# Attention forward and backward on one core: head strips at 32 rows, a shorter query-major exponential with DMA transposes for the rest, and gradient scores placed around the burst

## The chip, the cores and the metric

The kernel runs on one core of a Trainium2 chip. The time is device microseconds of one execution; the kernel before takes 2680.48 us in the median of 3 runs (2678.87 to 2681.03). The core has a matrix engine (PE, which loads weights through PEld), a vector engine (DVE), an activation engine (ACT), a general engine (POOL) and a queue engine (SP); DMA transfers are issued from SP, ACT and POOL.

## The reference

One layer mixes two branches with a gate, and the kernel returns the output and the gradients of eleven inputs. Only branch A matters here: attention over 2048 positions with 32 heads of width 18, forward and backward. The other branch, a state-space convolution, matters by one thing: its basis tables are built on POOL while the attention runs.

```python
g = sigmoid((x * gate_w).sum(-1, keepdims=True))
qkv = (x @ wqkv)                                # 32 heads, head width 18
scores = einsum("bhqd,bhkd->bhqk", q, k) * 18**-0.5
o = einsum("bhqk,bhkd->bhqd", softmax(scores), v)
out = g * (o @ wo) + (1 - g) * B(x, ...)        # B: the convolution branch
_out, _vjp = jax.vjp(f, A_x, A_wqkv, A_wo, ..., gate_w);  _grads = _vjp(grad_out)
```

## The kernel before

**Stages.** A first stage projects q, k and v and writes them to a DRAM tensor `QKV_d` as strips, one row for each head channel, 2048 positions long. The attention follows (from about 120 to 2100 us), then the convolution branch and the output projections.

**Units and steps.** Four heads form a group and occupy 32 partitions each. A *unit* is one group and one block of 512 queries; there are 8 groups x 4 blocks = 32 units (`NU`). A unit has 32 *steps* (`NST`); the loop over `G` runs through 1024 steps (`NTOT`), and the backward half trails the forward half by `OFF` = 39 steps, so one step works on two units at once:

- *P1*: scores with keys on partitions, for 128 keys, 512 queries and two heads. ACT turns them into exponentials, tile `PT` (L1388).
- *P3*: scores with queries on partitions, for 128 queries, 512 keys (block `kq`) and two heads. ACT turns them into exponentials, tile `eb` (L1393).
- *P2*: gradient scores, one for each of two heads; DVE multiplies each with `PT` into tile `ds` (L1398).
- the *burst*: one of eight slots, repeated for each `kq`: the gradient of V from `eb` and `dOa` (two halves, `dv_half`), of Q from `ds` (two halves), of K from `dsT` (two halves), and two slots that transpose on PE (`turn`). A second half or a turn ends with an eviction on DVE (`evs`).
- in half of the steps, four matmuls of the forward output `accO`.

`dsT` is `ds` transposed, for the most part by DMA transposes issued from SP (L1406). The K, V and Q tiles (`KaT`, `VaT`, `QaT`, `Vtok`, `Ktok`, `Qtok`) and the packing transposes `gT` are on the same SP queue.

**Order.** The program is written out by hand (`manual_schedule`): each engine takes its instructions in the order in which the loop body emits them, and waits at the first one that isn't ready. `at(("pre", G), f)` emits `f` ahead of step `G`. PSUM holds two P1/P3 tiles (tag `S`), two P2 tiles (tag `dP`), one burst accumulator (`accB`) and `accO`.

**Between forward and backward of a unit.** DVE takes the reciprocal `rl` (L1044) of the row sums; POOL multiplies `dOa` (L1049) and `prod` (L1051); DVE reduces `prod` (L1057), PE turns `dOa`, and P2 of that unit can begin.

**POOL.** Besides these two multiplications POOL builds the tables of the convolution branch: a fixed list of multiplications and additions (L506), their stores (`E_d<-Eo`, L559), and the packing of gradients (`dtk`, L1075, stored at L1076). `e_emit` spreads the list over the steps: at each `G` it emits as much as a cost estimate says is due. What it emits stands in POOL's queue ahead of the next unit's `dOa`.

Of the kernel before, what the change touches and what calls it, by code (L numbers as in the profile page):

```python
# [17 lines left out]
P = 128  # L18


def build(tc, aps, dbg_aps=None, stages=("s1", "attn", "post", "s4", "final")):
# [23 lines left out]
    HS = DH + 2  # L45
    assert HS <= HP and (4 * HS) % 16 == 0
# [15 lines left out]
    with ExitStack() as gctx:  # L62
# [14 lines left out]

        HR = H * HS
        QKV_d = dram.tile([2 * HR + H * HP, S], BF, name="QKV_d")
        ROW0 = {"K": 0, "V": HR, "Q": 2 * HR}  # L80
        WID = {"K": HS, "V": HS, "Q": HP}
# [44 lines left out]
        woT = [eds.tile([P, 2, 512], BF, tag="eb", bufs=8, name="eb").rearrange("p a b -> p (a b)")[:, 0:D] for _ in range(DC)]  # L126
        dO_st = [eds.tile([P, 2, 512], BF, tag="eb", bufs=8, name="eb") for _ in range(3)]

        with ExitStack() as ctx:
# [11 lines left out]
            rows = [QKV_d[ROW0[k_]:ROW0[k_] + H * WID[k_], :].rearrange("(h w) s -> h w s", w=WID[k_]) for k_ in "QKV"]  # L141
# [48 lines left out]
            def load_const():  # L190
                for q_, (y0, y1) in enumerate(((DH + 1, HP), (DH, HS), (DH, HS))):
                    nc.sync.dma_start(rows[q_][:, y0:y1, :], cst_d[q_:q_ + 1].unsqueeze(1).to_broadcast([H, y1 - y0, S]))
# [757 lines left out]
        if "attn" in stages:  # L950
# [3 lines left out]
            DA = HP  # L954
            NFILL = {"V": 1, "Q": 0, "K": 0}
            with ExitStack() as ctx:
# [28 lines left out]
                def strip(k, g, c0, n):  # L985

                    r0 = ROW0[k] + 4 * g * WID[k]
                    return bass.AP(tensor=QKV_d.tensor, offset=QKV_d[r0:r0 + 1, c0:c0 + 1].offset, ap=[[WID[k] * S, 4], [S, HP], [1, n]])

# [12 lines left out]
                def load_piece(nm, g, m):  # L1002
# [4 lines left out]
                    else:  # L1007
                        t_ = ga.tile([P, TPQ, P], BF, tag=nm, bufs=PB[nm], name=nm + "_g")
                        r0 = ROW0[k] + 4 * g * WID[k]
# [126 lines left out]
                def dv_half(g, b, kq, h, acc):  # L1136
                    U = UN[(g, b)]
                    for ii in (2 * h, 2 * h + 1):
                        for j in range(4):
                            mm(acc[HP * j:HP * (j + 1), :], lhsT=U["dOa"][:, ii, j, :], rhs=U["eb"].pop((kq, ii, j)),  # L1140
                               start=(ii == 0), stop=(ii == 3), tile_position=(0, HP * j))

# [11 lines left out]
                def dq_half(g, b, kq, h, acc):  # L1154
                    U = UN[(g, b)]
                    for n_ in (2 * h, 2 * h + 1):
                        for j in range(4):
                            mm(acc[HP * j:HP * (j + 1), :], lhsT=grp_t[g]["Ktok", kq][:, n_, HS * j:HS * j + HP], rhs=U["ds"][TPQ * kq + n_][:, j, :],
# [83 lines left out]
                at(("pre", 4), load_z01)  # L1242
# [632 lines left out]
```

## Time and profile before

| | |
|---|---|
| median of 3 runs | 2680.48 us |
| span of the profiled execution | 2673.6 us |
| mean granted TensorE clock | 0.968 |
| busy, of the span | PE 90%, DVE 86%, ACT 88%, POOL 68%, PEld 42% |
| from 400 to 700 us | PE 270.34, DVE 272.21, ACT 300.00, POOL 253.68 of 300 us |

The profiled execution's own time isn't listed apart from the three runs; its span, from the first to the last instruction, is 2673.6 us, 6.9 us less than their median. Busy shares are means over stages: in the attention ACT has no idle time, and in the stages behind it ACT has little to do. A row of the chain of waits gives a start, a length and what was running. A row of a timeline gives start, length, engine, line, operation, tiles and, in brackets, the idle time before it with what ended it. Instructions overlap in the pipeline of an engine, so the pace of a row of equal instructions is the distance of their starts, which is shorter than the length of one.

### The profile page before, as it was taken

What the parts mean: (1) busy time and instruction counts of PE and PEld (TensorE: products, weight loads), DVE (VectorE), ACT (ScalarE), POOL (GpSimd) and SP (SyncE); (2) the same over time, 40 slices, a digit from 0 to 9 for tenths busy, and PEclk for the clock granted to TensorE, in tenths of its full rate; (3) what the DMA queues carried; (4) which work ended last, traced back from release to release, by engine and by line L of the source; (5) the groups of instructions that cost most, each with busy time, mean ns of one, the idle gap of its engine ahead of it and who ended that gap; (6) DMA issues with size and microseconds to landing.
All of it is one profiled execution on the core that took longest, in us unless ns stands there. A gap on an engine that the chain in (4) does not pass through costs nothing.

```text
span 2673.6 us, 69952 instructions
## 1 busy us (share of the span) xinstructions
PE 2405.5 (90%) x27411; PEld 1134.6 (42%) x27411; DVE 2294.7 (86%) x4090; ACT 2352.0 (88%) x2744; POOL 1830.1 (68%) x2845
## 2 busy tenths in 40 slices
PE   8999999998889898889898999989988699999999
PEld 4433333333333333333333333333232489998756
DVE  5748999999889999889899999999897499999964
ACT  5589999999999999999999999999996489999321
POOL 0388878888888888888878888887931135555431
PEclk9989999999999999999999999999896699999999
DMA  7747889879979978997898899779668979998996
GB/s 232 202 114 152 150 171 177 162 156 181 169 151 172 185 157 163 173 167 152 165 179 157 157 172 169 154 164 181 134 136 174 224 229 262 260 263 250 269 255 136
DMA packets 1155478, 486.63 MB, mean 182 GB/s; under 512 B 1071062, under 2 KB 1108551, under 8 KB 1152843
## 3 DMA queue, kind: packets, MB, share of 16 engines
q1 hardware_dynamic: 1108346, 339.13, 64.3%
q0 software_dynamic: 44784, 137.52, 19.2%
q10 hardware_dynamic: 2016, 5.51, 0.7%
q8 instruction: 214, 3.51, 0.6%
q14 instruction: 118, 0.96, 0.1%
HBM read 146.27 MB, written 93.80 MB: 90 GB/s over the span
## 4 chain that ended last, share of the span: by engine, by line
ACT 39%; PE 28%; DVE 22%; issue 6%; DMA 3%; POOL 2%; SPq 1%; ACTq 0%; DVEq 0%; POOLq 0%
ACT eb L1393 23%; ACT PT L1388 14%; PE ps_P L30 8%; DVE ds L1398 7%; DVE tz L733 3%; DVE wab L753 3%; PE accV L30 2%; PE ps_dx L30 2%; PE turn_p L1097 2%; DVE tz L736 2%; PE accK L30 2%; DVE HG L738 2%; PE yp L30 2%; DVE Rw L758 1%; DVE dvacc L1151 1%
## 5 line engine op out<-in xcount | busy, mean ns | idle before, releaser
L1398 DVE TENSOR_TENSOR ds<-ps_P,PT 128x512 bf16<-128x512 f32 x2048 | 1312.5, 683 | 127.8 <-PE ps_P L30 87.3
L1393 ACT ACTIVATE eb<-ps_P 128x1024 bf16<-128x1024 f32 x1024 | 1095.7, 1070 | 44.3 <-PE ps_P L30 44.2
L1388 ACT ACTIVATE PT<-ps_P 128x1024 bf16<-128x1024 f32 x1024 | 1099.6, 1075 | 11.0 <-PE ps_P L30 9.5
L30 PE MATMUL ps_P<-dOaT,VaT_g 32*128 32x512 bf16 x2048 | 583.1, 390 | 30.8 <-DVE ds L1398 15.4
L506 POOL TENSOR_TENSOR et<-eG,eT 128x448 f32<-128x448 f32 x576 | 542.9, 963 | 10.7
L30 PE MATMUL ps_P<-QaT_g,KaT_g 32*128 32x512 bf16 x2048 | 404.7, 387 | 126.6 <-ACT PT L1388 122.2
L30 PE MATMUL ps_P<-KaT_g,QaT_g 32*128 32x512 bf16 x2048 | 408.9, 392 | 2.0 <-ACT eb L1393 1.4
L506 POOL TENSOR_TENSOR Eo<-et,et 128x448 bf16<-128x448 f32 x288 | 327.2, 1136 | 20.8
L30 PEld LDWEIGHTS <-KaT_g 32*128 32x128 bf16 x2048 | 147.4, 91 | 456.1 <-issue 438.2
L30 PEld LDWEIGHTS <-QaT_g 32*128 32x128 bf16 x2048 | 115.7, 91 | 288.6 <-issue 266.7
L30 PE MATMUL accV<-eb,dOa 128*32 128x512 bf16 x2048 | 185.6, 396 | 26.8 <-ACT eb L1393 26.5
L30 PE MATMUL accO<-PT,Vtok_g 128*32 128x512 bf16 x2048 | 207.9, 395 | 0.1
L30 PE MATMUL accK<-dsT,Qtok_g 128*32 128x256 bf16 x4096 | 165.3, 283 | 21.3 <-DMA dsT<-ds 19.9
L30 PE MATMUL accQ<-ds,Ktok_g 128*32 128x512 bf16 x2048 | 161.9, 394 | 2.2 <-DVE dvacc L1151 1.9
L30 PEld LDWEIGHTS <-Vtok_g 128*32 128x32 bf16 x2048 | 52.8, 93 | 222.6 <-issue 222.6
L1102 DVE COPY dsT<-turn_p 128x1024 bf16<-128x1024 bf16 (+1 forms) x216 | 139.2, 644 | 3.4 <-PE turn_p L1097 3.4
L1097 PE MATMUL turn_p<-ident_bf,ds 128*128 128x128 bf16 x1664 | 136.2, 225 | 1.4 <-DVE gb L1169 0.8
L672 ACT COPY E1e<-etp 128x1024 bf16<-128x1024 bf16 x132 | 125.4, 1063 | 2.7 <-PE etp L671 2.7
L30 PEld LDWEIGHTS <-Qtok_g 128*32 128x32 bf16 x4096 | 88.6, 97 | 87.8 <-issue 57.9
L506 POOL TENSOR_TENSOR et<-eT 128x32 f32<-128x32 f32 (+3 forms) x288 | 116.2, 424 | 11.4
L1097 PEld LDWEIGHTS <-ds 128*128 128x128 bf16 x1664 | 98.9, 100 | 50.2 <-issue 50.0
L1075 POOL COPY dtk<-gT 128x288 bf16<-128x288 bf16 x96 | 40.9, 426 | 107.6 <-DMA dqkv_d<-dtk 47.2
(295 smaller groups left out, 3731.0 us busy)
## 6 DMA issues: line engine op xcount, KB each, us to landing
E_d<-Eo POOLq DMA_DIRECT2D x144, 256.0 KB, 3.3
E1n<-E_d POOLq DMA_DIRECT2D x30, 1024.0 KB, 6.6
T0w<-Kp_d SPq DMA_DIRECT2D x18, 1024.0 KB
xs<-xb_d POOLq DMA_DIRECT2D x28, 512.0 KB, 9.9
dsT<-ds SPq DMA_TRANSPOSE x512
dqkv_d<-dtk POOLq DMA_DIRECT2D x96, 72.0 KB, 4.3
Md_d<-mst SPq DMA_DIRECT2D x18, 288.0 KB
skw<-Md_d SPq DMA_DIRECT2D x72, 64.0 KB
```

The costliest lines, as they stand in the source:

```text
L30: return nc.tensor.matmul(out, lhsT=lhsT, rhs=rhs, start=start, stop=stop, **kw)
L506: nc.gpsimd.tensor_tensor(out, a, b, op=op)
L672: copy(E_[:, 4 * q:4 * q + 4], pt_)
L733: nc.vector.tensor_tensor(tz[x], HG[:, :, k - 1].unsqueeze(1).to_broadcast([P, 2, 2, n, CB]), ZZ.unsqueeze(3).to_broadcast([P, 2, 2, n, CB ...
L736: nc.vector.tensor_tensor(tz[x][:, 0], tz[x][:, 0], UVk[:, :, :, k, :], op=A.add)
L738: nc.vector.tensor_tensor(HG[:, :, k], tz[x][:, 0], tz[x][:, 1, ::-1], op=A.add)
L753: nc.vector.tensor_tensor(wab, h_, w_, op=A.mult)
L1097: nc.tensor.transpose(pt_[:, x, qb, :], t_[:, qb * P:(qb + 1) * P], ident_bf)
L1102: (nc.scalar.copy if NTOT <= now[0] < NTOT + OFF else nc.vector.tensor_copy)(o_(), pt_[:, x:x + n])
L1388: nc.scalar.activation(U["PT"][i, j // 2], ps, ACT.Exp)
L1393: nc.scalar.activation(e, ps, ACT.Exp)
L1398: nc.vector.tensor_tensor(U["ds"][i][:, j, :], ps, U["PT"][i, j // 2][:, j % 2, :], op=A.mult)
```

## The change

1. Heads in the K and V strips of `QKV_d` stand 32 rows apart (`HP`) rather than 20 (`HS`); `strip` becomes a plain block of 128 rows, and the slices of `Vtok` and `Ktok` move to multiples of 32. The added constant rows are written for the first four heads from SP, and for the other 28 by two DMAs from POOL at steps 8 and 24 (`late_rows`).
2. P3 scores and their exponentials are 384 keys wide rather than 512 (`KT`). The last 128 keys of each 512-key block come from `PT`, which holds the same exponentials with keys on partitions: `turn_p` transposes a 128x1024 tile by DMA from SP, two for each `kq`, eight in a unit.
3. `dv_half` therefore has four matmuls 384 wide for each of two query tiles, and eight 128 wide from the transposed tile `PTt` between them.
4. The first P2 matmul of a step (`p2(0)`) goes between P1 and the burst, the second stays behind P3. The burst's eviction on DVE moves from ahead of the two multiplications to between them.

```diff
-        QKV_d = dram.tile([2 * HR + H * HP, S], BF, name="QKV_d")
+        HR = H * HP
+        QKV_d = dram.tile([3 * HR, S], BF, name="QKV_d")
...
-                for q_, (y0, y1) in enumerate(((DH + 1, HP), (DH, HS), (DH, HS))):
-                    nc.sync.dma_start(rows[q_][:, y0:y1, :], cst_d[q_:q_ + 1]...to_broadcast([H, y1 - y0, S]))
+                nc.sync.dma_start(rows[0][:, DH + 1:HP, :], cst_d[0:1]...)
+                for q_ in (1, 2):
+                    nc.sync.dma_start(rows[q_][0:4, DH:HP, :].rearrange("h w s -> w h s"), cst_d[q_:q_ + 1]...)
...
+                def turn_p(u, kq, pair):
+                    U = UN[u]
+                    t_ = U["PTt", kq, pair] = work.tile([P, 2 * TPQ, KR], BF, tag="PTt", bufs=2, name="PTt")
+                    nc.sync.dma_start_transpose(out=t_, in_=U["PT"][kq * TPQ + 3, pair][P - KR:P].rearrange("p x q -> p (x q)"))
...
+                    stored(2 * h)
+                    turned(2 * h)
+                    turned(2 * h + 1)
+                    stored(2 * h + 1)
...
+                def late_rows(q_):
+                    e_done[0] += 1.25
+                    nc.gpsimd.dma_start(qkv_rows[q_][4:H, DH:HP, :], cst_d[q_:q_ + 1]...to_broadcast([H - 4, HP - DH, S]))
+                for q_ in (1, 2):
+                    at(("pre", 16 * q_ - 8), lambda q_=q_: late_rows(q_))
...
+                            at(("pre", u_ * NST + OFF + 8 * kq_ + 1 + pair_), lambda ...: turn_p(units[u_], kq_, pair_))
...
+                    if r2:
+                        p2(0)
                     evs = []
...
-                            row(ps[:, x, :], T["QaT", b][:, ii * P:(ii + 1) * P], T["KaT", kq], jo + x)
+                            row(ps[:, x, 0:KT], T["QaT", b][:, ii * P:(ii + 1) * P], T["KaT", kq][:, 0:KT], jo + x)
...
+                        p2(1)
...
-                            e = eds.tile([P, 2, KB], BF, tag="eb", bufs=8, name="eb")
+                            e = eds.tile([P, 2, KT], BF, tag="eb", bufs=8, name="eb")
...
-                            nc.scalar.activation(e, ps, ACT.Exp)
+                            nc.scalar.activation(e, ps[:, :, 0:KT], ACT.Exp)
...
+                            if j % 2 == 0:
+                                for e_ in evs:
+                                    e_()
```

How this moves instructions. PE, the step with the first half of a V burst; `ps_P<-QaT,KaT` is P1, `<-KaT,QaT` is P3, `<-dOaT,VaT` is P2, and the weight loads and the repeats for further heads are left out. Before:

```order
L30 MATMUL ps_P_2680<-QaT_g,KaT_g 128x512
...
L30 MATMUL accV<-ident_bf,J_bf 128x512
...
L30 MATMUL accV<-eb,dOa_1232 32x512
...
L30 MATMUL ps_P_2693<-KaT_g,QaT_g 128x512
...
L30 MATMUL ps_P_2696<-dOaT,VaT_g 128x512
...
L30 MATMUL ps_P_2698<-dOaT,VaT_g 128x512
```

PE, the same place after:

```order
L30 MATMUL ps_P_3338<-QaT_g,KaT_g 128x512
...
L30 MATMUL ps_P_3341<-dOaT,VaT_g 128x512
...
L30 MATMUL accV<-ident_bf,J_bf 128x512
...
L30 MATMUL accV<-eb,dOa_1234 32x384
...
L30 MATMUL accV<-PTt,dOa_1234 32x128
...
L30 MATMUL accV<-eb,dOa_1234 32x384
...
L30 MATMUL ps_P_3361<-KaT_g,QaT_g 128x384
...
L30 MATMUL ps_P_3364<-dOaT,VaT_g 128x512
```

The first P2 stands ahead of the burst, P3 is narrower, and the burst reads the DMA transposes.

SP, within a unit of the middle of the attention, after (before, the same stretch has no row of `PTt`):

```order
L1442 DMA_TRANSPOSE dsT<-ds 128x12x128
L1116 DMA_TRANSPOSE PTt<-PT 128x8x128
L1442 DMA_TRANSPOSE dsT<-ds 128x12x128
L1012 DMA_TRANSPOSE Qtok_g<-QKV_d 128x4x128
L1116 DMA_TRANSPOSE PTt<-PT 128x8x128
L1073 DMA_TRANSPOSE gT<-dvacc 128x4x128
L1012 DMA_TRANSPOSE Ktok_g<-QKV_d 128x4x128
```

Two more transposes stand among the four `dsT` of each `kq`; a `dsT` behind them is issued later by as long as SP takes for them. DVE, an eviction of the V burst before, and then after:

```order
L1398 TENSOR_TENSOR ds<-ps_P_2998,PT 128x512
L1398 TENSOR_TENSOR ds<-ps_P_3000,PT 128x512
L1146 COPY dvacc<-accV 128x512
L1398 TENSOR_TENSOR ds<-ps_P_3025,PT 128x512
L1398 TENSOR_TENSOR ds<-ps_P_3027,PT 128x512
```

```order
L1431 TENSOR_TENSOR ds<-ps_P_3069,PT 128x512
L1431 TENSOR_TENSOR ds<-ps_P_3084,PT 128x512
L1163 COPY dvacc<-accV 128x512
L1431 TENSOR_TENSOR ds<-ps_P_3105,PT 128x512
L1431 TENSOR_TENSOR ds<-ps_P_3129,PT 128x512
```

After, the tiles 3084 and 3105 are the two of one step, and the eviction stands between them. POOL's own list keeps its length, two `late_rows` DMAs aside.

More of the change, by code (lines that the diff above doesn't have):

```diff
@@ L44, in build @@
     HP = 32
[L45 to L46 removed]
+    assert DH + 1 <= HP
     c_scale = float(DH) ** -0.5
@@ L1242, in build @@
                 at(("pre", 4), load_z01)
+                def late_rows(q_):
+                    e_done[0] += 1.25
+                    nc.gpsimd.dma_start(qkv_rows[q_][4:H, DH:HP, :], cst_d[q_:q_ + 1].unsqueeze(1).to_broadcast([H - 4, HP - DH, S]))
+                for q_ in (1, 2):
+                    at(("pre", 16 * q_ - 8), lambda q_=q_: late_rows(q_))
                 SLOTS = {0: ("V", dv_half, 0), 1: ("V", dv_half, 1), 2: ("Q", dq_half, 0), 3: ("Q", dq_half, 1), 5: ("K", dk_half, 0), 6: ("K", dk_half, 1)}
                 NTOT = NU * NST
+                for u_ in range(NU):
+                    for kq_ in range(NQ):
+                        for pair_ in range(2):
+                            at(("pre", u_ * NST + OFF + 8 * kq_ + 1 + pair_), lambda u_=u_, kq_=kq_, pair_=pair_: turn_p(units[u_], kq_, pair_))
                 def put_x(k):
@@ L1314, in build, with p2 @@
                         rows.append(("P1", g, b, i, j0, ps))
+                    def p2(x):
+                        g, b, s2 = r2
+                        i2, j2 = s2 // 2, 2 * (1 - (s2 + OFF) % 2) + x
+                        ps = apsp.tile([P, KB], F32, tag="dP", bufs=2, name="ps_P2")
+                        row(ps, grp_t[g]["VaT", i2 // TPQ][:, (i2 % TPQ) * P:(i2 % TPQ + 1) * P], UN[(g, b)]["dOaT"].rearrange("p t q -> p (t q)"), j2)
+                        rows.append(("P2", g, b, i2, j2, ps))
+                    if r2:
+                        p2(0)
                     evs = []
```

43 lines of the change are left out of this document (22 added, 21 removed).

## The prediction

> **What bounds the kernel now.** I read the page first (ACT 39% of the chain, 37% in the two exponentials), then one window over 29 units of the attention, from the first `dOa` of POOL to the thirtieth, then the waits of POOL in that window.
>
> ```profile
> ACT 39%; PE 28%; DVE 22%; issue 6%; DMA 3%; POOL 2%; SPq 1%; ACTq 0%; DVEq 0%; POOLq 0%
> ACT eb L1393 23%; ACT PT L1388 14%; PE ps_P L30 8%; DVE ds L1398 7%; DVE tz L733 3%; DVE wab L753 3%; PE accV L30 2%; PE ps_dx L30 2%; PE turn_p L1097 2%; DVE tz L736 2%; PE accK L30 2%; DVE HG L738 2%; PE yp L30 2%; DVE Rw L758 1%; DVE dvacc L1151 1%
> 169.60:1885.90 1716.30, 1543.98 (x16619) 537.24 (x16616) 1541.69 (x2540) 1708.65 (x1855) 1452.33 (x2382) 0.99 0.87 165
> 1007.11 1.04 ACT L1388 ACTIVATE PT<-ps_P 128x1024 bf16<-128x1024 f32 x1
> 1008.02 1.05 ACT L1393 ACTIVATE eb<-ps_P 128x1024 bf16<-128x1024 f32 x1
> 1008.92 1.07 ACT L1388 ACTIVATE PT<-ps_P 128x1024 bf16<-128x1024 f32 x1
> 2210.99 1.61 ACT L708 ACTIVATE UV<-uvp 128x512 bf16<-128x512 f32 x3
> L708 ACT ACTIVATE UV<-uvp x144: 587/616/663, 2113.0 to 2477.3; 128x512 bf16<-128x512 f32 x144
> ```
>
> The window's columns are PE, PEld, DVE, ACT, POOL busy, clock, DMA share, GB/s. A unit takes 1716.3/29 = 59.2 us. ACT is busy for 1708.65 of 1716.30: it bounds. Exponentials of 1024 columns start (1008.92-1007.11)/2 = 0.905 us apart, so 64 of them need 57.9 us a unit. DVE is busy 1541.69/29 = 53.2 us a unit.
>
> POOL looks free (1452 of 1716 us busy), but it is a queue, and what matters is where it waits:
>
> ```profile
> POOL dOa L1049 <- DVE rl L1044: 87.4, 25, 5.1
> POOL E_d L559 <- POOL Eo L506: 39.5, 133, 0.3
> POOL dtk L1075 <- DMA dqkv_d<-dtk: 34.6, 18, 5.6
> POOL dqkv_d L1076 <- POOL dtk L1075: 27.6, 84, 1.0
> 1885.77 0.67 POOL L1049 TENSOR_TENSOR dOa<-dO_b,rl 128x288 bf16<-128x288 bf16 x1
> 1948.21 0.68 POOL L1049 TENSOR_TENSOR dOa<-dO_b,rl 128x288 bf16<-128x288 bf16 x1 [8.33 <-DVE rl L1044]
> POOL dOa L1049 <- DVE rl L1044: 44.4, 2, 36.1
> ```
>
> Only the first row (waits, the same window; the last row is the same for 1886 to 2010) is a wait for the attention. The others are POOL's own work and stores and remain at any pace. So POOL needs (1716.3-87.4)/29 = 56.2 us a unit. It is 3.0 us behind ACT as a bound, and the busy shares don't show it.
>
> **The change part by part.**
>
> *Exponentials.* The 512-wide rows start (1.61-0.616)/2 = 0.497 us apart, so a column costs (0.905-0.497)/512 = 0.80 ns, and 768 columns cost 0.905-256x0.80 ns = 0.70 us. A step needs 1.605 us of ACT, a unit 51.4 us, 6.5 us less. ACT falls behind DVE (53.2 us) and POOL. DVE's work stays the same in number and width.
>
> *PE.* P3 loses a quarter of its columns; the V burst has the same columns in twice the matmuls, 16 in a half, as many as the K burst has. Below, a step with a K burst:
>
> ```profile
> 1884.91 0.39 PE L30 MATMUL ps_P<-QaT_g,KaT_g 32*128 32x512 bf16 x2
> 1885.23 0.62 PE L30 MATMUL accK<-dsT,Qtok_g 128*32 128x256 bf16 x16
> 1885.78 0.39 PE L30 MATMUL ps_P<-KaT_g,QaT_g 32*128 32x512 bf16 x2
> 1885.79 0.39 PE L30 MATMUL ps_P<-dOaT,VaT_g 32*128 32x512 bf16 x2
> 1886.10 0.40 PE L30 MATMUL accO<-PT,Vtok_g 128*32 128x512 bf16 x4
> 1886.44 0.39 PE L30 MATMUL ps_P<-QaT_g,KaT_g 32*128 32x512 bf16 x2
> ```
>
> From P1 to P1 are 1.53 us, 49 us a unit at most, so PE covers it: I take 0. P2 and P3 start 0.01 us apart, in other partitions, so they run side by side; `p2(0)` is in the half that P1 doesn't use and rides beside P1 in the same way. If that cover failed it would cost the 0.3 us that a further pass takes (1885.78 to 1886.10).
>
> *Order.* PE now waits for a P2 tile ahead of the burst, and behind that wait stand the burst and P3, on which ACT waits. The eviction releases `accB` one multiplication later, and the next burst waits for it. The old order loses 59.2-57.9 = 1.3 us a unit against its bound; I take the same beside DVE's 53.2: 54.5 us a unit for the attention without POOL. Bounds: 53.2, and 59.2 if the waits eat everything.
>
> *DMA transposes.* SP gets eight `PTt` a unit.
>
> ```profile
> L1406 SPq DMA_TRANSPOSE dsT<-ds x512: 1274/1458/5387, 175.8 to 2098.6; - x171
> L1071 SPq DMA_TRANSPOSE gT<-dkacc x32: 1188/1220/2568, 381.7 to 2104.5; - x32
> 1132.01 1.05 PE L30 MATMUL accK<-dsT,Qtok_g 128*32 128x256 bf16 x16 [1.85 <-DMA dsT<-ds]
> ```
>
> Between 1.22 us (512 columns) and 1.46 (mostly 1536): 1.35 us, or 10.8 us a unit. SP now issues 16 `dsT` (23.3), some 6 other transposes (7.5) and 5 loads and stores (about 0.55 each, 2.8 in all, an estimate): 34 us, after it 45 of 56. A `PTt` is issued five or six steps (9 us) ahead of its burst. I take 0; in the unit that ends a group, where up to nine `gT` stand in the queue, the third row shows that a late transpose already stops PE once. Bounds: 0, and 1.85 us with what follows for each `kq`.
>
> *POOL.* The list is the same. Two `late_rows` DMAs cost 0.61 us (the row below, the nearest store of constants) to some 1.3 us each, once: 1 to 3 us, under the first units' waits. K and V loads keep size and number; the constants from SP grow by two times 96 KB before the attention: 0 to 1 us.
>
> ```profile
> 1022.20 0.61 POOL L1259 DMA_DIRECT2D xb_d<-cst_d  x1
> ```
>
> So with 54.5 us for the attention POOL becomes the bound at 56.2, and DVE waits at L1057 for `prod`, 1.7 us in an average unit. What does such a wait cost? (First row: who waited for `prod` in the whole run before, us and times.)
>
> ```profile
>   DVE dOa L1057: 4.2, 3
> 703.63 0.46 DVE L1057 TENSOR_REDUCE dOa<-prod 128x16 bf16<-128x288 f32 x1 [1.38 <-POOL prod L1051]
> 1887.25 0.46 DVE L1057 TENSOR_REDUCE dOa<-prod 128x16 bf16<-128x288 f32 x1 [1.79 <-POOL prod L1051]
> 1888.35 0.38 PE L1097 MATMUL turn_p<-ident_bf,dOa 128*128 128x128 bf16 x4 [1.53 <-DVE dkacc L1183]
> 703.00:710.00 7.00, 5.31 (x53) 1.72 (x49) 5.98 (x11) 6.02 (x8) 6.52 (x9) 1.00 0.67 140
> 1889.00:1909.00 20.00, 19.83 (x151) 5.48 (x150) 13.90 (x23) 15.80 (x16) 18.36 (x22) 0.50 0.53 117
> 1131.00:1137.50 6.50, 5.49 (x49) 2.07 (x48) 3.74 (x6) 3.75 (x5) 4.05 (x7) 0.50 1.12 198
> ```
>
> After a wait of 1.38 us the granted clock stayed at 1.00; after 1.79 us, with PE idle for 1.53, it was 0.50 for 20 us, and after PE's 1.85 above for 6.5. Under 0.50 a step takes 20/8 = 2.5 us (16 exponentials), so 20 us lose 20x(1-1.70/2.5) = 6.4 us and 6.5 lose 2.1: 4.3 on average. It limits itself: the unit behind it takes 54.5+4.3 = 58.8 us, POOL catches up, and the next wait falls away. A pair of units then takes (58.8+56.2)/2 = 57.5. The average wait of 1.7 lies between the two rows, so I let half of them trip: (56.2+57.5)/2 = 56.85.
>
> The Trainium skill, in "TensorE: Matmul & The Clock Gate", section "HAM oscillation — how this bites in real kernels", says that the matrix engine keeps its clock as long as no idle gap is longer than about 3.4 us. By that no such wait trips, which is the second rival's time, 2588. The traced gaps of 1.53 and 1.85 us did trip, so I don't go by it.
>
> *The last two units.* POOL's list thins out; from 1885.8 to 2007.0 they took 121.2 us and take 2x54.5 plus 1: 11 us less.
>
> *The tail.* Without P1, `p2(0)` has nothing to ride beside:
>
> ```profile
> 2008.00:2045.00 37.00, 33.81 (x284) 10.79 (x282) 27.98 (x45) 22.16 (x23) 3.59 (x8) 0.50 0.69 135
> 2030.82 0.61 PE L30 MATMUL ps_P<-dOaT,VaT_g 32*128 32x512 bf16 x2
> 2031.36 0.62 PE L30 MATMUL accV<-eb,dOa 128*32 128x512 bf16 x4
> ```
>
> At clock 0.50 a pass takes 0.54 us (from 2030.82 to 2031.36), and with 45 DVE instructions at about 2.6 a step some 17 steps lie in that stretch: 0 to 9 us lost. PE is idle there for 37-33.81 = 3.2 us, which can cover a part: I take 6.
>
> **Sum.** 29x(59.2-56.85) = 68, plus 11, minus 6: 73 us less. The profiled span of 2673.6 becomes 2601, and with the 6.9 us by which the median stands above it, 2608.
>
> **The rivals.**
> - *POOL doesn't hold.* If the attention could run past it: 29x4.7+11-6 = 141: 2540; if POOL only loses its 34.6 us of waits for `dqkv_d`: 2555. Against it: `dOa` stands in POOL's queue behind the list, and those waits are POOL's own.
> - *POOL holds, but no wait trips the clock.* 29x3.0+11-6 = 92: 2588. For it: the row of 703.63, and that DVE's waits come before PE's tiles run out; against it: the row of 1887.25.
> - *SP is late.* In the eight units that end a group transposes come late, as at 1132.01, for each of four `kq`: 8x4x(1.85+2.1) = 126 us, of which POOL, which is slow in the same units (the late rows of 703.63 and 1887.25 are such units), hides an estimated half: 63 of the 73 us go, 2671. For it: 5.39 us, the longest issue of a `dsT`.
> - *Slower.* The same lateness in every unit. With a share f of the steps at 2.5 us, 1.70+0.8f reaches 59.2/32 = 1.85 at f = 0.19, some 11 us of half clock in a unit: two trips of 6.5. Three trips a unit (20 us, f = 0.34) give 1.97 a step, 63 us a unit: 2790. For it: PE's wait for `dsT` and the shared queue; against it: 11 us of SP free in a unit.
> - *The change doesn't shorten ACT.* The 512-wide rows speak against it.
>
> **How the numbers follow.** POOL as the bound with some trips (2595 to 2645, its own range): 0.45, predicted 2608. No trips (2575 to 2595) 0.15; POOL not the bound (below 2575) 0.09; SP late in group ends (2645 to 2675) 0.17; within 0.2% 0.04; slower 0.10. 0.2% (5 us) is about what a measurement of this kernel tells from no change. The range 2570 to 2683 leaves out some 0.08 below and 0.11 above. Faster is 0.45+0.15+0.09+0.17 = 0.86, same 0.04, slower 0.10.
>
> **What would show it.** In the profile after: `eb` rows 128x768 starting 0.70 us before the next; POOL's waits at L1049 nearly gone, DVE's wait for `prod` at L1057 grown from 4.2 us in the whole run to tens; ACT with idle time; some stretches of 0.50 behind these waits. It is wrong if PE waits for `PTt` or `dsT` often, if ACT still has no idle time, or if units get shorter than 56 us.

## The result and the profile after

The change makes the kernel slower: 2690.53 us in the median of 5 runs (2688.48 to 2701.50) against 2678.87 before (5 runs beside them), a ratio of 1.0056 with an interval of 1.0034 to 1.0079. 2608 was predicted, in a range of 2570 to 2683. The profiled execution has a span of 2686.8 us (before 2673.6): 13.2 us more.

The page of the changed kernel: busy time of PE, DVE, ACT and POOL, the granted clock and the share of the DMA engines in 40 slices, the queue from which SP's transfers run (packets, MB, share of 16 engines), and the chain.

```profile
PE 2370.2 (88%) x29459; PEld 1167.2 (43%) x29459; DVE 2281.0 (85%) x4090; ACT 2166.0 (81%) x2744; POOL 1832.3 (68%) x2847
PEclk9977997898889799879987988998998699999999
DMA  7759999999999999999999999999999979998996
q1 hardware_dynamic: 1379430, 406.21, 80.9%
PE 13%; DVE 10%; ACT 4%; DMA 3%; SPq 2%; issue 1%; DVEq 0%; ACTq 0%; POOL 0%
```

ACT idles 19% of the span (12% before), as intended. The chain can't be set beside the one of before, in which ACT had 39%: its shares add up to 33% of the span, since it leads back only to 1787.9 us, and of most of the attention it says nothing. No compute engine took ACT's place at full use, and the clock digits fall below 9 again and again through the attention. Only the DMA digits stand at 9 in all of it, and the queue has 80.9% of the engines' time where it had 64.3%.

The attention by its units: POOL's first, thirtieth and last `dOa` (timeline; in brackets what POOL waited for), and the window of 29 units between the first two (PE, PEld, DVE, ACT, POOL busy, clock, DMA share, GB/s).

```profile
189.20 0.67 POOL L1051 TENSOR_TENSOR dOa<-dO_b,rl 128x288 bf16<-128x288 bf16 x1 [23.67 <-DVE rl L1046]
1907.09 0.68 POOL L1051 TENSOR_TENSOR dOa<-dO_b,rl 128x288 bf16<-128x288 bf16 x1 [3.60 <-DVE rl L1046]
2014.09 0.67 POOL L1051 TENSOR_TENSOR dOa<-dO_b,rl 128x288 bf16<-128x288 bf16 x1 [28.39 <-DVE rl L1046]
189.20:1907.10 1717.90, 1514.90 (x18420) 562.75 (x18416) 1528.51 (x2538) 1541.13 (x1852) 1453.71 (x2378) 0.90 1.10 200
```

With the same `dOa` of before at 168.93, 1885.77 and 2006.97, the 13.2 us lie here:

| us | before | after | moved | predicted |
|---|---|---|---|---|
| start of the span to first `dOa` | 168.9 | 189.2 | +20.3 | 0 to +1, `late_rows` under other waits |
| 29 units | 1716.8 | 1717.9 | +1.1 | -68 |
| last two units | 121.2 | 107.0 | -14.2 | -11 |
| from there to the end | 666.6 | 672.7 | +6.1 | +6 |

In the row of before the clock was 0.99 and the DMA share 0.87; now 0.90 and 1.10 (a share above 1: packets of several queues are in one engine at the same time).

Who waits in that window (us, times, longest us):

```profile
ACT eb L1426 <- PE ps_P L30: 142.1, 197, 4.5
DVE ds L1431 <- PE ps_P L30: 119.7, 144, 4.6
POOL dOa L1051 <- DVE rl L1046: 87.2, 21, 23.7
PE accV L30 <- DMA PTt<-PT: 42.8, 29, 3.7
PE accK L30 <- DMA dsT<-ds: 20.3, 11, 4.1
DVE dOa L1059 <- POOL prod L1053: 4.4, 5, 1.3
```

ACT and DVE wait for PE, PE waits for DMA transposes, and POOL waits for the attention: POOL has not become the bound, since DVE hardly ever waits for `prod`. One such stop, on SP and PE, and the windows before and behind it:

```profile
729.04 1.26 SPq L1116 DMA_TRANSPOSE PTt<-PT  x1
730.40 5.35 SPq L1442 DMA_TRANSPOSE dsT<-ds  x1
735.86 1.25 SPq L1116 DMA_TRANSPOSE PTt<-PT  x1
740.72 0.40 PE L30 MATMUL accV<-PTt,dOa 128*32 128x128 bf16 x6 [2.98 <-DMA PTt<-PT]
727.00:737.70 10.70, 9.55 (x122) 3.73 (x120) 10.54 (x19) 10.70 (x14) 10.06 (x12) 1.00 1.02 182
740.70:760.70 20.00, 19.98 (x181) 6.11 (x184) 13.87 (x22) 14.48 (x17) 15.46 (x34) 0.52 0.98 193
```

One `dsT` takes SP 5.35 us to issue. The second `PTt` stands behind it, is issued at 737.11 and needs another 3.6 us in the full DMA engines. PE stands for 2.98 us; then the clock is halved for some 20 us, in which ACT and DVE are busy for 14 of 20. Summed over the rows of the granted clock, half clock covers 358 us between the first and the last `dOa`, in 31 stretches of 11.6 us on average; before it was 55 us.

### The profile page after: what moved, and what is told of

Its sections match the earlier page's. It is cut to its first block, busy times and chain, and to the rows that moved or that the text cites. A ratio compares the mean times of both kernels' runs of the same rounds, so it can differ in the third digit from the quotient of the medians.

```text
span 2686.8 us, 74662 instructions
## 1 busy us (share of the span) xinstructions
PE 2370.2 (88%) x29459; PEld 1167.2 (43%) x29459; DVE 2281.0 (85%) x4090; ACT 2166.0 (81%) x2744; POOL 1832.3 (68%) x2847
## 3 DMA queue, kind: packets, MB, share of 16 engines
q1 hardware_dynamic: 1379430, 406.21, 80.9%
## 5 line engine op out<-in xcount | busy, mean ns | idle before, releaser
L1421 ACT ACTIVATE PT<-ps_P 128x1024 bf16<-128x1024 f32 x1024 | 1084.4, 1060 | 53.4 <-PE ps_P L30 52.4
L1426 ACT ACTIVATE eb<-ps_P 128x768 bf16<-128x768 f32 x1024 | 861.9, 842 | 196.7 <-PE ps_P L30 185.8
L30 PE MATMUL ps_P<-dOaT,VaT_g 32*128 32x512 bf16 x2048 | 815.1, 414 | 5.1 <-DVE ds L1431 4.9
L30 PE MATMUL ps_P<-QaT_g,KaT_g 32*128 32x512 bf16 x2048 | 454.4, 413 | 103.0 <-ACT PT L1421 98.7
L30 PE MATMUL ps_P<-KaT_g,QaT_g 32*128 32x384 bf16 x2048 | 368.1, 356 | 0.9 <-ACT PT L1421 0.5
L506 POOL TENSOR_TENSOR Eo<-et,et 128x448 bf16<-128x448 f32 x288 | 327.3, 1136 | 20.7
L30 PEld LDWEIGHTS <-QaT_g 32*128 32x128 bf16 x2048 | 98.4, 92 | 280.3 <-issue 260.0
L30 PE MATMUL accV<-eb,dOa 128*32 128x384 bf16 x2048 | 190.9, 367 | 17.9 <-ACT eb L1426 9.3
L30 PEld LDWEIGHTS <-VaT_g 32*128 32x128 bf16 x2048 | 181.1, 92 | 2.5 <-issue 2.4
L30 PEld LDWEIGHTS <-dOa 128*32 128x32 bf16 x4096 | 88.4, 100 | 206.6 <-issue 195.6
L30 PE MATMUL accV<-PTt,dOa 128*32 128x128 bf16 x2048 | 88.8, 237 | 51.3 <-DMA PTt<-PT 51.1
L1099 PEld LDWEIGHTS <-ds 128*128 128x128 bf16 x1664 | 104.6, 104 | 56.2 <-issue 56.1
```

What stands on the lines that cost most here:

```text
L30: return nc.tensor.matmul(out, lhsT=lhsT, rhs=rhs, start=start, stop=stop, **kw)
L506: nc.gpsimd.tensor_tensor(out, a, b, op=op)
L1099: nc.tensor.transpose(pt_[:, x, qb, :], t_[:, qb * P:(qb + 1) * P], ident_bf)
L1421: nc.scalar.activation(U["PT"][i, j // 2], ps, ACT.Exp)
L1426: nc.scalar.activation(e, ps[:, :, 0:KT], ACT.Exp)
```

## The experiments

The theory after the result: **A**, the `PTt` transposes overload what issues and moves them (SP, the DMA engines), so that `PTt` and `dsT` land late and stop PE; **B**, without that POOL would be the bound; **D**, the start is lost to `late_rows`. The rivals: the new order of P2 and the burst, the 32-row strips, or a bound that already stands at 59 us. "Units" below are the average of the first 29, "half clock" is the sum within the attention.

### What the transposes cost: e1, e5, e8

**e1_no_turn.** Without the transposes; the burst reads constants.

```diff
-    at(("pre", u_ * NST + OFF + 8 * kq_ + 1 + pair_), lambda ...: turn_p(...))
-    mm(acc[...][KT:KB], ..., rhs=U["PTt", kq, j // 2][:, j % 2 * TPQ + ii, :], ...)
+    mm(acc[...][KT:KB], ..., rhs=PTc[j // 2][:, j % 2 * TPQ + ii, :], ...)
```

> The changed kernel without its 256 DMA transposes of PT: the 128-wide V matmuls read two constant tiles instead, so the last quarter of each key block of the V gradient is left out. All instructions of PE, ACT and DVE stay. Theory A (the DMA transposes reach PE late, PE stops, and each stop halves its clock): PE's waits for PTt and most of those for dsT go, half clock falls from 358 us of the attention to under 100, and the time is 2605 to 2630, POOL being the next bound at 56.2 us a unit. Rival C (the narrower or reordered work of PE lowers the clock by itself): 2680 to 2695, half clock stays above 300 us.

Measured: 2598.43 us, ratio 0.9688 (0.9659 to 0.9718). Units 56.35 us, half clock 174 us. The window of the 29 units, and the waits for `prod` and `dsT` (from 190 to 1840 us):

```profile
192.13:1826.42 1634.29, 1451.81 (x18462) 554.37 (x18458) 1520.91 (x2541) 1531.59 (x1855) 1450.16 (x2378) 0.95 0.91 173
DVE dOa L1064 <- POOL prod L1058: 41.4, 20, 3.8
PE accK L30 <- DMA dsT<-ds: 2.0, 2, 1.7
```

Theory A is right in kind, since rival C's 300 us of half clock are not there, and missed both of its numbers: half clock is 174 us and not under 100, and the time is 7 us below its range. The kernel that was predicted is this one: DVE waits for POOL 20 times, and a unit takes 56.35 us where 56.2 to 56.85 was worked out. All that is missing from the forecast's units comes with the transposes.

**e5_tiny_turn.** As many transposes at the same places, with an eighth of the columns, into a tile that nobody reads; the burst reads constants, as in e1.

```diff
-    t_ = U["PTt", kq, pair] = work.tile([P, 2 * TPQ, KR], ...)
-    nc.sync.dma_start_transpose(out=t_, in_=U["PT"][kq * TPQ + 3, pair][P - KR:P].rearrange("p x q -> p (x q)"))
+    t_ = work.tile([P, 1, KR], BF, tag="PTs", bufs=2, name="PTs")
+    nc.sync.dma_start_transpose(out=t_, in_=U["PT"][kq * TPQ + 3, pair][P - KR:P, 0, 0:KR])
```

> The changed kernel whose 256 transposes of PT are kept at their places in SP's queue but carry an eighth of the columns (128x128 into a tile that nobody reads); the matmuls of the last quarter of the V gradient read constants, so that quarter is left out of the result. Without any PT transposes it took 2598.4 us, SP was busy for 0.69 of the attention, and half clock covered 174 us of it; with them 2690.5, 0.92 and 358 us. Theory A1 (SP's own issue time is what makes the transposes late: it is paid per instruction, at 1.2 us even for small ones, as the gT rows of 1.19 us suggest): SP busy 0.85 to 0.90, dsT still late, PE stops for dsT of 5 us or more in all, 2640 to 2680 us. Theory A2 (the DMA queues' bandwidth is: the packets that a transpose moves): SP at about 0.75 to 0.85 without stops for dsT, 2595 to 2615 us. Between the two: 2615 to 2640, both share in it.

Measured: 2615.69 us, 0.9789 (0.9747 to 0.9831). SP was busy for 0.88 of the attention and PE stopped for `dsT` 15 times for over 0.9 us, 37 us in all, as A1 said; the time is where both would share, at A2's edge. Its DMA share, and the length of these transposes on SP (min/median/max ns):

```profile
300.00:1800.00 1500.00, 1318.78 (x16806) 508.40 (x16806) 1385.75 (x2313) 1388.23 (x1681) 1313.71 (x2144) 0.95 0.96 177
L1121 SPq DMA_TRANSPOSE PTs<-PT x256: 1119/1184/2881, 187.9 to 2023.1; - x128
```

**e8_unread_turn.** The transposes at full size and at their places, but the burst reads `ident_bf` instead of `PTt`.

> The changed kernel with all 256 transposes of PT at full size and at their places, but no matmul reads them: the last quarter of the V gradient multiplies a constant and is left out of the result. Without the transposes it took 0.969 of the kernel before, with transposes of an eighth of the size that nobody reads 0.979, and with everything 1.006. Theory A3 (most of the loss is PE standing at the burst for a PTt that landed late): the stops at accV are gone, 0.98 to 0.985 of the kernel before, 2620 to 2638 us, half clock about 200 us. Theory A4 (the loss is the load that the full transposes put on SP and the DMA queues, whoever reads them): dsT comes late instead, SP busy 0.91 or more, half clock above 280 us, 2660 us or more. Between: both.

Measured: 2680.25 us, 1.0028 (1.0005 to 1.0051); half clock 270 us, SP busy 0.93. Theory A4 holds, with some 10 us less of half clock than it asked for, and A3 falls. The window from 300 to 1800 us, and the wait for `dsT` from 190 to 1900:

```profile
300.00:1800.00 1500.00, 1286.15 (x16302) 495.35 (x16303) 1345.94 (x2241) 1348.95 (x1630) 1276.81 (x2077) 0.93 1.13 202
PE accK L30 <- DMA dsT<-ds: 85.5, 39, 6.0
```

Nobody waits for `PTt`, but now `dsT` is late: 85.5 us. So the loss is the load itself, whoever is hit by it. In steps of the ratio: the issues with an eighth of the bytes 0.969 to 0.979 (27 us), the other bytes 0.979 to 1.003 (64 us), reading them 1.003 to 1.006 (8 us, or 14 by the second measurement of the changed kernel below; the intervals of this last step overlap).

### What would bound the kernel next: e2

**e2_no_turn_light.** As e1, and POOL's list without the four multiplications of each row; its two additions only write a constant.

```diff
-    eops.append((1.02, lambda mul=mul, ri=ri, st=st: mul(0, ri, st)))
-    eops.append((1.02, lambda mul=mul, ri=ri, st=st: mul(1, 1 - ri, st)))
+    eops.append((1.02, lambda: None))
+    eops.append((1.02, lambda: None))
```

> As the kernel without transposes, and POOL's list is shortened: the four multiplications of each basis row are left out and its two additions are stores of a constant (about 5 us less for each of 144 rows, 720 us of POOL). Theory B (POOL's list bounds a unit at 56.2 us once ACT is faster): 40 to 70 us less than the kernel without transposes, units at 53.2 to 55 us. Rival (PE, DVE and ACT bound each other there, POOL is hidden): within 10 us of it.

Measured: 2548.42 us, 0.9504 (0.9463 to 0.9544). Units 54.44 us, where the forecast had 54.5 for the attention without POOL. In its window of 29 units:

```profile
189.38:1768.08 1578.70, 1412.43 (x18420) 551.36 (x18416) 1516.14 (x2538) 1524.99 (x1852) 767.43 (x1846) 0.98 0.97 179
```

POOL is busy for 767 us instead of 1450 and DVE for 1516 of 1579: DVE is the bound. B holds: POOL's list is what comes next.

### The order of P2 and the burst: e4

**e4_order_only.** The kernel before with `p2(0)` ahead of the burst and the eviction behind the first multiplication, and nothing else of the change.

> The kernel before with the fourth part of the change alone: P2 split around the burst, the eviction between the two multiplications; exponentials 512 wide, no transposes of PT, strips at 20 rows. Theory A (the order is harmless while ACT bounds): 2679 to 2690, the loss of up to 9 us being in the last unit, where P2 alone takes a further pass at half clock. Rival E (the order itself makes PE wait for DVE and ACT): above 2695, with ACT idle in the attention.

Measured: 2679.18 us, 0.9996 (0.9978 to 1.0013). The order costs nothing and brings nothing while ACT is the bound, the tail included (666.8 us behind the last `dOa`, before 666.6). The 6.1 us of the changed kernel's tail are not its doing alone.

### The start: e3, e11, e13

In the changed kernel's start DVE cannot take a staging tile because a store of `dO_d` has not landed, and PE stands behind it (timeline, then windows from the start of half clock):

```profile
141.42 0.46 DVE L1240 CAST eb<-ps_dO 128x288 bf16<-128x288 f32 x1 [6.11 <-DMA dO_d<-eb]
141.93 1.47 PE L30 MATMUL ps_dO<-eb,ds 128*128 128x288 bf16 x6 [5.21 <-DVE eb L1240]
164.70 1.47 PE L30 MATMUL ps_dO<-eb,ds 128*128 128x288 bf16 x6 [4.73 <-DVE eb L1240]
138.90:149.00 10.10, 7.07 (x30) 2.37 (x29) 2.10 (x5) 3.08 (x3) 9.48 (x16) 0.50 0.43 90
162.70:180.00 17.30, 15.29 (x66) 5.00 (x65) 3.84 (x9) 7.17 (x7) 2.45 (x3) 0.51 0.37 98
```

**e11_strips_only.** The kernel before with the first part of the change alone: strips at 32 rows, and `late_rows`.

> The kernel before with the first part of the change alone: strips at 32 rows, late_rows; exponentials at 512, no PT transposes, order as before. Theory D (the two large writes cost the start some 17 to 20 us and ACT, which bounds every unit at 59.2 us, can't win them back): first dOa at 185 to 192 us, units 59.2 us, 1.005 to 1.008, which would be all of the changed kernel's loss. Rival (the late start is caught up later, or strips at 32 rows make the units shorter): 1.000 to 1.003.

Measured: 2684.60 us, 1.0033 (1.0014 to 1.0052). First `dOa` at 192.6, just past the 192 of D; but the units are shorter than before, and the ratio lies between the ranges of D and of its rival:

```profile
192.58:1899.71 1707.13, 1535.63 (x16579) 535.17 (x16578) 1537.59 (x2537) 1705.19 (x1852) 1450.47 (x2378) 0.99 0.84 165
```

1707.1 instead of 1716.8 us, with a DMA share of 0.84 instead of 0.87. In both kernels most units take 58.9 us; the kernel before has three of about 62, e11 none above 59.9, and half clock covers 20 us of its attention where it was 55. So in these profiles the part costs 23.7 us at the start and gives 10 back.

**e3_late_const.** The changed kernel with `late_rows` as fourteen small transfers, two for each group, some 20 steps ahead of its loads.

```diff
-    nc.gpsimd.dma_start(qkv_rows[q_][4:H, DH:HP, :], ...)
+    nc.gpsimd.dma_start(qkv_rows[q_][h0:h0 + 4, DH:HP, :], ...)
...
+    at(("pre", 4 * NST * (n_ - 1) + 44 + 4 * q_), lambda q_=q_, n_=n_: late_rows(q_, 4 * n_))
```

> The changed kernel with the constant rows of heads 4 to 31 written in fourteen small POOL transfers, two for each group, one group ahead of their use, instead of two of 1.6 MB at steps 8 and 24. Theory D (the two large writes hold up dO_d stores at the start, DVE and PE wait, and the first 39 steps take 17 us longer): 12 to 20 us less, about 2674. Rival (the start is late for another reason, such as the clock): 2688 to 2693.

Measured: 2709.24 us, 1.0099 (1.0057 to 1.0141). The start is repaired (first `dOa` at 175.1), but units take 60.1 us. D was right on the start and wrong on the time; why small transfers hurt the units this much stays open.

**e13_late_later.** The two transfers as they are, at steps 42 and 54 instead of 8 and 24.

```diff
-    at(("pre", 16 * q_ - 8), lambda q_=q_: late_rows(q_))
+    at(("pre", 12 * q_ + 30), lambda q_=q_: late_rows(q_))
```

> The changed kernel with its two late_rows transfers at steps 42 and 54 instead of 8 and 24, behind the start and ahead of the loads that read them. If the start loss is theirs and nothing else comes of them: first dOa at 171 to 176 us, units 59.0 to 59.5 us, 0.998 to 1.002. Rival (what the start gains is lost in the first units, as with the fourteen small transfers): units of 59.8 us or more, 1.004 to 1.011.

Measured: 2687.02 us, 1.0048 (1.0023 to 1.0073); first `dOa` at 178.1, units 59.98 us, the first of them 65.0 (in the changed kernel 54.1). The profiled execution lies 16 us above the median. The start's gain is lost in the first unit. The same happens in e14 and e15 (below), which have the same transfers. The second transfer of e14, and the longest stop of that unit:

```profile
205.85 0.75 POOL L1263 DMA_DIRECT2D QKV_d<-cst_d  x1
224.88 0.29 PE L30 MATMUL accV<-PTt,dOa 128*32 128x128 bf16 x2 [7.10 <-DMA PTt<-PT]
```

PE stands for 7.1 us from 12 us behind the issue of that 1.6 MB write, which took POOL 0.75 us. That the write delayed this `PTt` is argued from its place, since no later unit has such a write or a stop of that length; it was not tried apart.

### The strips: e6, e9, e12

**e6_rows20.** The changed kernel with K and V strips at 20 rows a head and their constants as before; no `late_rows`.

> The changed kernel with only its first part undone: the K and V strips at 20 rows a head with their constants written as before, and no late_rows transfers; exponentials at 384 keys, transposes and order as changed. Theory D (the start loses some 17 to 20 us to the two large late_rows writes, and nothing gives it back later): first dOa at 170 to 176 us instead of 189, units as in the changed kernel (59 to 59.5 us on average), 2668 to 2677 us. Rival D2 (the attention is bound by SP and DMA in all, so that what the start gains is lost in the following units, as with the fourteen small transfers): units 59.8 us or more on average, 2683 to 2695 us.

Measured: 2715.28 us, 1.0157 (1.0115 to 1.0198): slower than either theory had it. The start is back (first `dOa` at 175.6), but the units take 60.9 us. The profiled execution lies 16 us above the median.

**e9_rows20_ballast.** The same with the two `late_rows` transfers, now into a tensor that nobody reads.

> The changed kernel with the strips at 20 rows, which took 1.016 of the kernel before although its attention began 14 us earlier than the changed kernel's; here the two late_rows transfers are kept in shape and place, but go to a scratch tensor that nobody reads. Theory P (what sets the pace of the units is how the attention lies in time against POOL's list and its DMAs, which a late start shifts): the start is late again, first dOa at 187 to 192 us, units 59.0 to 59.6 us, about 1.003 to 1.009, as the changed kernel. Rival L (the 20-row layout of the strips itself makes the units slower, by its loads): first dOa as late, units still 60.5 us or more, 1.018 or more.

Measured: 2728.37 us, 1.0211 (1.0173 to 1.0250); first `dOa` at 189.0, units 60.7 us. Rival L holds: it is the strips, not the place of the attention in time.

**e12_changed_again.** The changed kernel a second time, as a control.

> The changed kernel itself, beside the kernels of this call. If the 1.006 holds on any chip: 1.003 to 1.009, units of 59.2 us. If the chip made the difference to the versions with strips at 20 rows: 1.013 or more, units above 60 us.

Measured: 2693.77 us, 1.0082 (1.0050 to 1.0114), units 58.9 us. The first `dOa` is at 196.4 where the first profile had 189.2; over all profiles with these two transfers at steps 8 and 24 it lies between 184.7 and 196.4, so the start of a single profile is uncertain by some 6 us. By the profiles strips at 32 rows are worth 1.5 to 2 us a unit in the changed kernel, and 0.3 in the kernel before; by the ratios, 1.0211 of e9 against 1.0056 and 1.0082, it is 35 to 42 us in all, 1.1 to 1.3 a unit. The queue of SP's transfers from 300 to 1800 us (packets, MB, share of 16 engines), of e9:

```profile
q1 hardware_dynamic: 974939, 247.62, 99.0%
```

of the changed kernel:

```profile
q1 hardware_dynamic: 1009410, 255.97, 98.5%
```

of the kernel before:

```profile
q1 hardware_dynamic: 794215, 202.97, 74.6%
```

and of e11:

```profile
q1 hardware_dynamic: 799058, 203.75, 72.1%
```

A packet takes 0.990 x 16 x 1500/974939 = 24.4 ns with 20 rows and 23.4 ns with 32, 4% less at the same bytes each; between the kernel before and e11 it is 22.5 and 21.7 ns. Other versions with 32 rows and all transposes have up to 24.0 ns (e3), so the gain lies between 1.5 and 4%. Why packets are longer beside strips of 20 rows was not tried.

### Versions with fewer transposes: e7, e10, e14, e15

**e7_half_pair.** e6's strips; only the second pair of heads is 384 wide and transposed, four `PTt` a unit. The lines are set against e6.

```diff
-    for pair_ in range(2):
+    for pair_ in (1,):
...
-    row(ps[:, x, 0:KT], ..., T["KaT", kq][:, 0:KT], jo + x)
+    row(ps[:, x, 0:(KT if jo else KB)], ..., T["KaT", kq][:, 0:(KT if jo else KB)], jo + x)
```

> Strips at 20 rows a head as before; only the second pair of heads of each group has exponentials 384 keys wide and its last quarter transposed, the first pair keeps 512: four PT transposes a unit instead of eight. ACT then needs 32 x (0.905 + 0.905 + 0.70 + 0.905) / 2 = 54.6 us a unit, under POOL's 56.2. Theory A+B (SP has room for half of the transposes, at 0.92 - 0.12 = 0.80 busy, and POOL's list is the next bound): units of 56.2 to 57.0 us, half clock within the attention under 200 us, 2590 to 2620 us, faster than both kernels. Rival (SP is late already with half of them, or the bursts of 12 matmuls a half cost PE what they save): half clock above 250 us, units of 58 us or more, 2650 us or more.

Measured: 2661.92 us, 0.9947 (0.9920 to 0.9974): faster than both kernels, but with the half clock of the first theory (164 us) and the units (58.6 us) and the time of the rival. Most units take 56.4 to 57.6 us; the first of each later group, in which SP also has the last `gT` of the group ahead, takes 60 to 66.

**e10_half_pair32.** The same with strips at 32 rows and `late_rows` as in the change.

> The changed kernel (strips at 32 rows, late_rows as in it) with only the second pair of heads at 384 keys: four PT transposes a unit. With strips at 20 rows this took 0.995 of the kernel before. If strips at 32 rows help the units, as the 1.016 against 1.006 of the two full versions suggests, by some 1.5 us a unit less some 17 us at the start: 0.985 to 0.990. If only the late start is added: 1.000 to 1.003.

Measured: 2659.94 us, 0.9948 (0.9928 to 0.9969); units 58.3 us, half clock 133 us. The strips bring only 0.3 us a unit here, 9 us in the 29 units, against a start that is 20.7 us later (190.4). The medians of e7 and e10 are alike all the same; e10's profiled execution lies 8 us above its median.

**e14_half32_later.** e10 with the two transfers at steps 42 and 54.

> One pair at 384 keys (four full PT transposes a unit), strips at 32 rows, late_rows at steps 42 and 54. With the early late_rows it took 0.995. If the start comes back whole (14 to 17 us): 0.987 to 0.990; if not, 0.995.

Measured: 2652.32 us, 0.9922 (0.9895 to 0.9950), the fastest of the versions that leave nothing out. The start comes back (168.9), and the first unit takes 66.4 instead of 55.0 us, by the stop shown above.

**e15_one_head_later.** e14 with one head instead of one pair: ACT's second tile is 896 wide, four transposes a unit at half the bytes.

```diff
-    w_ = KT if j else KB
+    w_ = 2 * KB - (KR if j else 0)
...
-    nc.scalar.activation(e, ps[:, :, 0:w_], ACT.Exp)
+    nc.scalar.activation(e, ps.rearrange("p x q -> p (x q)")[:, 0:w_], ACT.Exp)
```

> As the kernel with one pair, but only one head of it at 384 keys: ACT's second exponential is 896 wide, 32 x (0.905 + 0.905 - 0.05) = 56.3 us a unit for ACT; the four PT transposes a unit stay in SP's queue at half their bytes. If the bytes on the DMA engines set the loss (their share was 0.87 before, 1.01 with one pair, 1.11 with both): share about 0.95, half clock under 80 us, units 57.3 to 57.9 us, 0.979 to 0.985. If the number of transposes in SP's queue does: half clock as with one pair (130 to 160 us), units 58.3 us or more, 0.988 to 0.992.

Measured: 2670.58 us, 0.9989 (0.9964 to 1.0014). In part as the first theory said: the DMA share is 0.94 and half clock 99 us, less than with one pair (167). But most units take 57.7 us, with ACT busy for 0.98 of the 29 units, the first takes 64.1, and the time is the kernel before's. With fewer bytes there was less half clock, and ACT gave up as much: a unit takes 58.7 us in both. Of the 14 us by which this profile is longer than e14's, 8 stand at the start (first `dOa` at 177.0 and 168.9), and their cause is open.

Share, clock and units side by side (share of the DMA engines from 300 to 1800 us; half clock within the attention):

| kernel | PT transposes a unit | DMA share | half clock, us | unit, us | ratio |
|---|---|---|---|---|---|
| before | 0 | 0.87 | 55 | 59.2 | 1 |
| e1, read constants | 0 | 0.92 | 174 | 56.4 | 0.969 |
| e5, an eighth | 8 | 0.96 | 198 | 57.0 | 0.979 |
| e15, one head | 4, half size | 0.94 | 99 | 58.7 | 0.999 |
| e14, one pair | 4 | 1.01 | 167 | 58.7 | 0.992 |
| changed | 8 | 1.11 | 358 | 59.2 | 1.006 |
| e8, unread | 8 | 1.13 | 270 | 59.0 | 1.003 |

Half clock alone does not set a unit's time: e1 and e14 have nearly the same and differ by 2.3 us a unit, and e8 has 88 us less than the changed kernel with units that are only 0.2 us shorter.

## Why the prediction was wrong

The sum missed by 86 us: 69 in the 29 units, 20 at the start, less 3 in the last two units.

**Exponentials: right.** Worked out were 0.70 us for 768 columns; ACT's rows start 0.69 us apart:

```profile
1479.39 0.82 ACT L1426 ACTIVATE eb<-ps_P 128x768 bf16<-128x768 f32 x1
1480.08 1.04 ACT L1421 ACTIVATE PT<-ps_P 128x1024 bf16<-128x1024 f32 x1
```

**Order and PE's cover: right.** e4 shows the order at no cost, e2 the attention at 54.44 us against 54.5. The 1.3 us of waits in this 54.5 were carried over from the old order, so to meet it within 0.1 us is in part luck.

**DMA transposes, "I take 0": the step that failed.** It priced each `PTt` by its issue on SP, 1.35 us, and set SP at 45 of 56 us. Its rows after:

```profile
L1442 SPq DMA_TRANSPOSE dsT<-ds x512: 1357/1650/5670, 195.4 to 2108.8; - x171
L1116 SPq DMA_TRANSPOSE PTt<-PT x256: 1231/1275/5115, 191.1 to 2093.2; - x128
```

The median of a `PTt` is under what I took. But the median `dsT` went from 1.46 to 1.65 us and its mean from 1.71 to 1.92 (I had costed it by the median), and SP's rows fill 0.92 of the attention, 54 us of a unit, not 45. Before the change they already filled 38.8 us of a unit and not 34, mostly because of the median, too. What drove them up was in the window that I quoted and never used: the DMA engines' share was 0.87 at 165 GB/s, which is 165 x 59.2 = 9.8 MB a unit. Eight `PTt` of 128x1024 bf16 are 2.1 MB, 21% more: 0.87 x 1.21 = 1.06 at the old pace and 1.10 at 56.85 us a unit. 1.10 at 200 GB/s was measured. A resource at 0.87 had no room for a fifth more at a faster pace, and e1, e5 and e8 show that the issues with an eighth of the bytes cost 27 us and the other bytes 64. SP's queue alone tells the same: 74.6% of 59.2 us are 44.2 us a unit before, and eight `PTt`, 8192 packets of 256 bytes at 22.5 ns on 16 engines, add 11.5. These 55.7 us would have taken up nearly all of the 56.85 of the forecast; 98.5% of 59.24, 58.4 us, were measured.

**The rival "SP is late"** named the mechanism and the queue behind which it acts, but kept it to the eight units at the end of a group and gave 2671. PE stood for late transposes in 18 of the 29 units. Still, the rival's place was the worst: the seven of these units in the window, those like the one of 1132.01, take 65.0 us on average (58.1 in e1), the other 22 take 57.4 (55.8). They have 48 of the 84 us between e1 and the changed kernel, and half of PE's waits for transposes. More of SP's packets fall into them, as in the unit from 1133.7 to 1204.0 us and the next one, to 1258.4 (packets, MB, share of 16 engines):

```profile
q1 hardware_dynamic: 44767, 11.34, 90.6%
q1 hardware_dynamic: 35875, 9.24, 102.1%
```

**The rival "slower"** had the break-even at some 11 us of half clock a unit; 358 us over 31 units are 11.6, and the 29 units took 59.24 us against 59.20. On average its working held, and its chance of 0.10 was too low; that the lateness is the same in every unit, as it had it, is not so.

**POOL: a right number that did not come to act.** 56.2 us a unit were measured in e1 as 56.35, with DVE waiting for `prod` as foreseen. In the changed kernel POOL still waits 87.2 us at L1051, since the units are no shorter than before. The forecast's 56.85 was an upper price of the trips there: e1 has 174 us of half clock (14.5 trips of 13.25 us, as forecast, are 192) and still 56.35.

**The clock.** I expected stops by POOL to halve it; in the changed kernel stops by transposes did. Of the 28 idle gaps of PE of 0.9 us or more at full clock in the changed kernel's attention, all 21 of 1.21 us or more were followed by half clock within 4 us, and of the seven below that one (1.02 us). It is no sharp bound: in the second profile of the changed kernel a gap of 1.69 us went by without it, in e14 one of 1.25, and nine of the 31 stretches had no gap of 0.9 us ahead of them. Two of the gaps, and the windows behind (PE, PEld, DVE, ACT, POOL busy, clock, DMA share, GB/s):

```profile
456.83 0.29 PE L30 MATMUL accV<-PTt,dOa 128*32 128x128 bf16 x6 [1.09 <-DMA PTt<-PT]
456.80:464.80 8.00, 6.98 (x96) 2.66 (x99) 7.02 (x12) 7.21 (x10) 7.45 (x9) 1.00 1.18 210
1680.86 0.29 PE L30 MATMUL accV<-PTt,dOa 128*32 128x128 bf16 x6 [1.21 <-DMA PTt<-PT]
1682.00:1690.00 8.00, 7.88 (x69) 2.18 (x62) 6.08 (x10) 6.29 (x8) 7.37 (x11) 0.59 1.10 243
```

The Trainium skill, "TensorE: Matmul & The Clock Gate", section "HAM oscillation — how this bites in real kernels", lets the clock be as long as no gap is longer than about 3.4 us; all but two of the 22 gaps that tripped here were shorter, so the trace does not agree. By the forecast's price (1 - 1.70/2.5 = 0.32 of the time at half clock) the 304 us more of it cost 97 us, more than the 69 that the units missed by. PE's waits for `PTt` and `dsT`, 63 us in the 29 units, come beside it, and parts of both are hidden behind other work; how the 69 us divide between them is not shown.

**`late_rows`, "1 to 3 us, under the first units' waits": wrong** by the same mistake: each was priced by its 0.6 to 1.3 us on POOL, and nothing was set for the 1.6 MB that it writes. The cost was 20.3 us, in e11 23.7, each of a single profile and uncertain by some 6.

**Last two units: right** in kind, -14.2 against -11. **Tail: a right number by luck**, +6.1 against +6. It was to come from P2 running alone. But e1 has the order, the P3 and the burst of the changed kernel, and its tail is 665.2 us, 1.4 shorter than before. All seven profiles with eight full transposes a unit have 671.2 to 681.8 us, the three with the same order and none or small ones (e1, e2, e5) 665.2 to 671.6. So the load of the transposes is the likelier cause, and that P2 alone costs anything is not shown.

## What to carry to other kernels

Price a DMA twice, by its issue on the queue and by its bytes on the shared DMA engines, and read the share column for the second: at 0.87 a fifth more bytes did not fit, and what came late was not only the transfer that was added but also the one beside it on the queue, even when nobody read the added one (e8). A stop of PE of little more than 1.2 us was followed by some 12 us of half clock here, so a transfer that is late by a microsecond is not a small thing. When one engine is relieved, measure the kernel with the price of the relief taken out, as in e1 and e2: that shows at once whether the next bound or the price has eaten the gain.

## What the runs showed of the hardware

- The granted clock halved within 4 us of every PE stop of 1.21 us or more at full clock in the profile of the changed kernel's attention; a stretch of half clock lasted 11.6 us on average. Single stops of 1.25 us (e14) and 1.69 us (the second profile of the changed kernel) went by without it.
- SP's queue, with packets of 254 bytes on average, nearly all of them transposes, took 98.5% of the time of the DMA engines for 255.97 MB in 1500 us, 171 GB/s. In a single unit its share was 102.1%, so packets of one queue overlap too, and the share is no strict limit. The Trainium skill, "DMA: Bandwidth & Descriptors", section "Latency and other measured facts", has 261 GB/s for DMA transposes with a non-contiguous middle dimension; from 300 to 1800 us this queue moved no more than 171 in any run.
- A transpose took SP 1.18 us in the median at 128 columns (e5) and 1.30 at 1024 (e8): in this case the issue hardly depended on the size, while the time of the kernel did, 0.979 against 1.003.
- Packets of the same size took 1.5 to 4% less time where K and V strips had 32 rows a head instead of 20.
- Beside two writes of 1.6 MB, each under a microsecond of its issuer's time, stores of `dO_d` kept DVE waiting for up to 6.1 us; with the writes moved away (e13, e14) or cut up (e3) the first `dOa` came 11 to 21 us earlier.
